# The first stage of x in 24 stores of 128 partitions, and the modes' preparation behind the second quarter's transposes

## The chip, the cores and the metric

The kernel runs on one core of one Trainium2 chip. Five engines work side by side, each with its own queue of instructions: TensorE (PE in the profile, its weight loads PEld), VectorE (DVE), ScalarE (ACT), GpSimd (POOL) and SyncE (SP). SP, ACT and POOL also issue DMA transfers. The metric is the device time of one execution in microseconds (us); the time of a kernel is the median of its runs.

## The reference, cut to what matters

The input `A_u` is one sequence of 2048 tokens with 448 channels, in float32. Two branches work on the same layer-normalised input, and their results are added to the input:

```python
xn = layernorm(x)
# branch A: a state-space model with 256 modes per channel, as a long convolution
K  = 2 * Re(sum_n C[d,n] * dt[d] * exp(A[d,n] * dt[d] * l))       # [448, 2048]
yA = irfft(rfft(xn, 4096) * rfft(K, 4096))[:2048] + xn * D_skip
# branch B: a gated unit, 448 -> 1792 -> 448
yB = (sigmoid(xn @ w_gate) * (xn @ w_up)) @ w_down
out = x + yA + yB
```

## The kernel before, in words

Tokens lie on partitions in blocks: 16 blocks `b` of 128 tokens, in four quarters of four blocks. A quarter is loaded, normalised on VectorE and ScalarE (`x_stats`, `x_scales`, `x_norm`), transposed on TensorE and split into a high part `xh` and a low part `xl` (`x_transpose`; the last 64 channels go to `xr`, whose lower half line 225 makes on VectorE). Products in float32 are made of three products of such halves. In the code `xls` holds that last line-225 instruction of the quarter transposed last.

Branch B is `glu`: for each of 14 tiles `f` of 128 hidden units and each quarter, `gate` runs 22 matmuls (line 710) into two PSUM banks `gu`, ScalarE takes the tanh (`th`), VectorE forms `hf` (line 721) and `hl` (728), ScalarE `hh` (726). A group of tiles then goes through line 823 into `po`, which line 828 adds to `acc`. The banks `gu` and `po` are four buffers in turn, so TensorE can go on only when VectorE has read an old one. The first two quarters come first ("half 0"), then the other two.

Branch A is `conv`. It runs in three stretches.

- **Preparation** (`prep`, lines 305 to 433, twice, for two halves of the channels): from the modes' parameters come powers and phases, by some 40 VectorE instructions on 112x512 tiles (for instance `ex` line 309, `fr` lines 315 and 316, a polynomial `pl` line 320) and ScalarE functions beside them.
- **The long filter** (`kgen`): 56 steps. Each makes magnitudes on GpSimd (line 520), phases on TensorE and ScalarE (`tr` line 542, `S` lines 548 to 551), products on VectorE (`Et`, `Ft`, lines 602 to 604) and 64 small matmuls (line 616). The phases are loaded 8 DMAs at a time (line 492).
- **The spectra** (`spectra`): 17 steps that load one part of the transformed x (`sx`, line 875), of the transformed filter (`skl`, 879) and a table (`tb`, 877), multiply them (`there`), transform back (`back`) and turn the result through DRAM (`v_d`, `vp`). Three loads are kept ahead (`NLD`).

The transformed x, named `x1_d` (`x_d` in the profile), is made early and kept in DRAM until the spectra. For the first two quarters `x_spec` (lines 283 to 305) makes it for two blocks at a time: four products, three copies on ScalarE, then the stores of line 301, issued on ScalarE's queue. For the other two quarters `pair_first` (lines 681 to 694) does the same with four copies (line 689) and the stores of line 691. In DRAM a block and group has its own row of 64 x 224 (`row`).

Two generators, `conv` and `glu`, are run in turn by weights, and a scheduler then sets the order on each engine by its own estimate of durations. `tc.issue_after(i)` holds instructions behind `i` in that order; `hp` raises a priority. Since the scheduler orders the whole program anew, an edit also shifts instructions far from it. Each DMA issued by SP or ACT signals one of eight semaphores, in rotation, and a new issue waits for the transfer that used that semaphore before; these are the names DMAHW0 to DMAHW7 in the order below.

Of the kernel before, what the change touches and what calls it, by code (L numbers as in the profile page):

```python
# [11 lines left out]
F32 = mybir.dt.float32  # L12
# [12 lines left out]
NB = 64  # L25
# [14 lines left out]
H = D // 2  # L40
# [8 lines left out]
LAG = 3  # L49
# [81 lines left out]
def s4d_glu_kernel(ctx, tc, io):  # L131
    nc = tc.nc
# [6 lines left out]
    dram = ctx.enter_context(tc.tile_pool(name="dram", bufs=1, space=DRAM))  # L139
    acc_d = dram.tile([128, 8, D], F32, name="acc_d")  # L140
    ph_d = dram.tile([D, 6, N], F32, name="ph_d")
    x1_d = dram.tile([2, NB, 64, H], F32, name="x1_d")

    sk_d = dram.tile([128, 2, 8, D // 64, 128], F32, name="sk_d")
    wt_d = dram.tile([2, NFT, 128, 8 * 128], F32, name="wt_d")
# [126 lines left out]
            return nc.scalar.activation(xn, xt, AF.Identity, bias=z_, scale=y_)  # L272

    def row(b, g):
        return 32 * (b // 4 % 2) + 8 * g + 4 * (b // 8) + b % 4

    def x_first_stage(to, xn, g):

        s = slice(32 * g, 32 * g + 32)
        for i in range(2):  # L280
            nc.tensor.matmul(to[64 * i : 64 * i + 64], wx[s], xn[i][s], start=True, stop=True)

    def x_spec(xn, b0):

        x1s_ = []
        for _ in range(2):
            x1s_.append(slots[("x1a", "x1b", "x1c")[x1s[0] % 3]])
            x1s[0] += 1
        ps = psc[-1].tile([128, 2, 512], F32, name="tr", bufs=1)
        kk = [psc[-1].tile([128, 512], F32, name=n, bufs=1) for n in ("ko", "kp")]  # L290
        with tc.issue_after(glu_mm[0].ins):
            for j in range(4):
                x_first_stage((ps[:, j] if j < 2 else kk[j - 2])[:, :D], xn, j)
        nc.scalar.copy(x1s_[0], ps[:, :, :D])
        for j in range(2):
            nc.scalar.copy(x1s_[1][:, j], kk[j][:, :D])
        for p in range(2):
            for i in range(2):
                r = row(b0 + i, 2 * p)
                for h in range(2):  # L300
                    nc.scalar.dma_start(
                        x1_d[h, r : r + 9 : 8].rearrange("r k d -> k r d"),
                        x1s_[p][64 * i : 64 * i + 64, :, H * h : H * h + H],
                    )
        yield 2 * WX

    def exp(ex, ki, fr, pl):
# [373 lines left out]
    def pair_first(b, xns):  # L681

        x1 = pg.tile([128, 2, D], F32, name="x1", tag="wraw", bufs=1)
        pss = [psg.tile([128, 512], F32, name="gu", bufs=4) for _ in range(4)]
        for g in range(4):
            x_first_stage(pss[g][:, :D], xns, g)
        for g in range(4):
            to = x1[:, g] if g < 2 else pg.tile([128, D], F32, name="x1", tag="rd", bufs=RB)
            nc.scalar.copy(to, pss[g][:, :D])
            for i in range(2):  # L690
                nc.scalar.dma_start(
                    x1_d[:, row(b + i, g)].rearrange("h k d -> k h d"),
                    to[64 * i : 64 * i + 64].rearrange("k (h d) -> k h d", h=2),
                )

    def gate(w, xs, to, between=None, behind=False):
        wh, wl = w
# [147 lines left out]
    def spectra(pf):  # L845
# [19 lines left out]
        def loads(h, k):  # L865
            sx = pf.tile([128, 4, H], F32, name="sx", bufs=NLD)
            sk = pf.tile([128, 7, 4, 32], F32, name="skl", bufs=NLD)
            if k == 32:

                nc.sync.dma_start(sx[:64, 0:2], x1_d[:, :, 32].rearrange("h b d -> b h d"))  # L870
                for i in range(2):
                    nc.sync.dma_start(sk[:64, :, i], sk_d[64:, i, 0, :, :32])
                return t32, sk, sx
            for i in range(2):
                nc.sync.dma_start(sx[64 * i : 64 * i + 64], x1_d[h, :, 32 * i + k : 32 * i + k + 4])
            tb = pf.tile([128, 4, 128], F32, name="tb", bufs=NLD)
            nc.sync.dma_start(tb, io["c_tab"][k // 4])

            nc.sync.dma_start(sk.rearrange("p g k e -> p g (k e)"), sk_d[:, h, k // 4])
            return tb, sk, sx  # L880
# [139 lines left out]
    def conv():  # L1020
        with tc.tile_pool(name="psk", bufs=1, space=PSUM) as ps_, tc.tile_pool(
            name="pq", bufs=1, side="right"
# [8 lines left out]
            with tc.tile_pool(name="pst", bufs=1, side="right", reuse_waits="tile") as pst:  # L1031
# [54 lines left out]
                while preps:  # L1086
                    for p in list(preps):
                        try:
                            with tc.issue_after(hfs[max(0, len(hfs) - LAG)].ins):
                                next(p)  # L1090
                        except StopIteration:
                            preps.remove(p)
                    yield WP
                    n += 1
                    if n in (2, 3):
                        if n == 2:
                            slots["x1c"] = pst.tile([128, 2, D], F32, name="x1c", tag="raw1")
                        for b in range(0, 4, 2):
                            yield from x_spec([xns[n - 2][:, b + i] for i in range(2)], 4 * (n - 2) + b)
# [11 lines left out]
    lasts, glu_mm, sp_mm, glu_on, outs, x1s, hfs, xls = [], [], [], [], [0], [0], [], []  # L1111
# [7 lines left out]
    while any(g is not None for g in gens):  # L1119
# [3 lines left out]
        i = min(live, key=lambda i: done[i] / total[i])  # L1123
# [33 lines left out]
```

## Time and profile before

| | us |
|---|---|
| median of 3 runs | 725.56 |
| lowest and highest run | 721.6, 726.61 |
| the profiled execution | 721.87 |
| its span, first to last instruction | 720.1 |

The profiled execution lies near the lowest of the three runs, 3.69 us under their median, and 1.77 us of it lie outside the span. Its mean granted TensorE clock is 0.984 of full speed. In the profile a time stands as microseconds from the start of the span; "x3" counts merged instructions; the bracket at the end of a row is how long the engine had been idle, and what ended the wait. ACTq and SPq are the queues in which ScalarE and SyncE issue DMAs.

### The profile page before, as it was taken

To read this page: it belongs to the slowest core of one execution; us is meant where nothing else is said; L and a number is where in the kernel's file an instruction comes from. 1 tells how busy PE (TensorE), PEld (TensorE's weight loads), DVE (VectorE), ACT (ScalarE), POOL (GpSimd) and SP (SyncE) were. 2 spreads that over 40 slices of the span, in tenths; PEclk is the share of its full clock that TensorE was granted. 3 is DMA by queue.
4 is the path that set the end of the run, shared out by engine and by line. 5 is a ranking of instruction groups with operands and counts; after the bars stand their busy time and mean duration, and the time that the engine had idled before them with its cause. 6 is when DMAs were issued, how large, how long until landed. Compare 5 with 4: busy or idle time off the path is not lost.

```text
span 720.1 us, 19127 instructions
## 1 busy us (share of the span) xinstructions
PE 670.9 (93%) x7752; PEld 527.3 (73%) x7752; DVE 551.4 (77%) x766; ACT 428.0 (59%) x678; POOL 371.5 (52%) x431
## 2 busy tenths in 40 slices
PE   3898999999997997989999999999999999998995
PEld 2676888877876875656888788877877777776783
DVE  5899988699899889985879889987946555546543
ACT  3655975677787789965686877777542322313320
POOL 2100147766987988885676687577833002251001
PEclk9999999999999999999999999999999999999998
DMA  9947374554254453647933344141359988899645
GB/s 208 238 118 215 97 214 154 166 159 153 64 168 140 135 135 107 178 136 203 257 112 95 95 132 128 46 140 43 86 162 319 216 235 231 253 290 228 172 131 152
DMA packets 94503, 117.23 MB, mean 163 GB/s; under 512 B 12752, under 2 KB 78288, under 8 KB 94416
## 3 DMA queue, kind: packets, MB, share of 16 engines
q1 hardware_dynamic: 65904, 91.87, 45.3%
q10 hardware_dynamic: 25936, 18.24, 9.5%
q0 software_dynamic: 2576, 5.90, 3.1%
q8 instruction: 61, 1.00, 0.6%
q14 instruction: 26, 0.21, 0.1%
HBM read 72.13 MB, written 43.84 MB: 161 GB/s over the span
## 4 chain that ended last, share of the span: by engine, by line
PE 42%; DVE 6%; ACT 4%; DMA 3%; issue 2%; SPq 1%; POOL 0%; POOLq 0%; DVEq 0%; ACTq 0%
PE gu L710 16%; PE po L823 9%; PE sp L904 6%; PE pv L931 4%; PE ko L616 4%; PE tr L542 2%; DVE Ft L604 1%; DMA sx<-x_d 1%; DVE Et L602 1%; DMA out_dram<-ac 1%; DVE Et L603 1%; PE kp L566 1%; ACT S L551 1%; ACT S L548 1%; SPq L492 1%
## 5 line engine op out<-in xcount | busy, mean ns | idle before, releaser
L520 POOL TENSOR_TENSOR me<-me,pm 128x32 f32<-128x32 f32 (+1 forms) x168 | 142.4, 848 | 73.4 <-DVE Et L603 62.1
L520 POOL TENSOR_TENSOR mf<-mf,pm 128x64 f32<-128x64 f32 (+1 forms) x112 | 119.7, 1069 | 5.9
L710 PE MATMUL gu<-xh,wh 128*128 128x512 f32 x336 | 100.0, 406 | 0.7 <-ACT xh L221 0.7
L710 PE MATMUL gu<-xh,wl 128*128 128x512 f32 x336 | 97.0, 395 | 0.0
L710 PE MATMUL gu<-xl,wh 128*128 128x512 f32 x336 | 95.8, 391 | 0.0
L602 DVE TENSOR_TENSOR Et<-me,S 128x1024 f32<-128x1024 f32 x56 | 81.8, 1461 | 17.2 <-ACT S L551 16.1
L603 DVE TENSOR_TENSOR Et<-me,S 128x1024 f32<-128x1024 f32 x56 | 78.0, 1394 | 12.6 <-ACT me L533 10.5
L823 PE MATMUL po<-dh,hh 128*128 128x448 f32 x224 | 84.2, 376 | 2.6 <-DVE hf L721 2.2
L823 PE MATMUL po<-dl,hh 128*128 128x448 f32 x224 | 82.3, 367 | 0.0
L604 DVE TENSOR_TENSOR Ft<-mf,S 128x1024 f32<-128x1024 f32 x56 | 78.1, 1394 | 5.4 <-ACT S L551 2.7
L548 ACT ACTIVATE S<-tr 128x1024 f32<-128x1024 f32 x56 | 57.6, 1028 | 40.8 <-PE tr L542 40.4
L823 PE MATMUL po<-dh,hl 128*128 128x448 f32 x224 | 81.2, 367 | 0.0
L616 PEld LDWEIGHTS ko<-Et,Ft 128*32 128x32 f32 x3584 | 55.2, 112 | 31.4 <-DVE Ft L604 13.3
L710 PEld LDWEIGHTS gu<-xh,wh 128*128 128x128 f32 x336 | 61.8, 191 | 20.1 <-issue 5.1
L616 PE MATMUL ko<-Et,Ft 128*32 128x64 f32 x3584 | 65.6, 224 | 10.8 <-DVE Ft L604 9.9
L710 PEld LDWEIGHTS gu<-xh,wl 128*128 128x128 f32 x336 | 63.8, 190 | 14.5 <-DVE hf L721 0.7
L710 PEld LDWEIGHTS gu<-xl,wh 128*128 128x128 f32 x336 | 63.4, 189 | 13.5
L726 ACT CAST hh<-hf 128x512 fp32r<-128x512 f32 x56 | 34.9, 623 | 61.8 <-DVE hf L721 57.7
L721 DVE SCALAR_TENSOR_TENSOR hf<-th,gu 128x512 f32<-128x512 f32 x56 | 38.1, 680 | 39.5 <-PE gu L710 27.1
L551 ACT ACTIVATE S<-S,hpi 128x1024 f32<-128x1024 f32 x56 | 65.5, 1170 | 0.0
L787 POOL TENSOR_TENSOR dl<-rd,dh 128x448 fp32r<-128x448 f32 x14 | 24.8, 1769 | 78.1 <-ACT dh L786 67.6
L828 DVE SCALAR_TENSOR_TENSOR acc<-po,acc 128x448 f32<-128x448 f32 x80 | 48.1, 615 | 20.7 <-PE po L823 20.4
(208 smaller groups left out, 1299.7 us busy)
## 6 DMA issues: line engine op xcount, KB each, us to landing
sk_d<-sk ACTq DMA_DIRECT2D x14, 512.0 KB
sx<-x_d SPq DMA_DIRECT2D x32, 224.0 KB
skl<-sk_d SPq DMA_DIRECT2D x16, 448.0 KB
vp<-v_d SPq DMA_DIRECT2D x16, 448.0 KB
v_d<-vt SPq DMA_DIRECT2D x14, 448.0 KB
ph<-ph_d SPq DMA_DIRECT2D x224, 24.0 KB
wt_d<-wh SPq DMA_DIRECT2D x9, 512.0 KB
wt_d<-wl SPq DMA_DIRECT2D x9, 512.0 KB
```

The costliest lines, as they stand in the source:

```text
L520: ins = nc.gpsimd.tensor_tensor(m[:, :, w + a : 2 * w : n], m[:, :, a:w:n], par(base + i).unsqueeze(2).to_broadcast([128, 4 * DC, w // n]) ...
L548: nc.scalar.activation(rows(cs), pv, AF.Abs)
L551: sins[:] = [nc.scalar.activation(cs, cs, AF.Sin, scale=-TWO_PI, bias=hpi)]
L602: v.tensor_tensor(Et[:, :, :, 32:64], two(me[:, :, 32:64]), S[:, 1::-1], ALU.mult)
L603: v.tensor_tensor(Et[:, :, :, 0:32], two(me[:, :, 0:32]), S[:, 1:3, :, ::-1], ALU.mult)
L604: fts[:] = [v.tensor_tensor(Ft, two(mf), S[:, 3:5], ALU.mult)]
L616: mm = nc.tensor.matmul(ko[32 * j : 32 * j + 32, sl], Ft[:, cc, DC * h + 4 * q + j], Et[:, cc, DC * h + 4 * q + j], start=(k == 0), stop=( ...
L710: glu_mm[:] = [nc.tensor.matmul(ps, a_, b_, start=(n == 0), stop=(n == len(mm) - 1))]
L721: marks[1] = v.scalar_tensor_tensor(hf, th, 1.0, pgu[1], ALU.add, ALU.mult)
L823: glu_mm[:] = [nc.tensor.matmul(po, a_[:, bs], w_, start=(n == 0), stop=(n == 3 * fc - 1))]
L828: v.scalar_tensor_tensor(acc[:, b], po, 0.5, acc[:, b], ALU.mult, ALU.add)
L904: mm = nc.tensor.matmul(to, tb[:kk, t, 64 * c : 64 * c + 64], rhs, start=True, stop=True, skip_group_check=True,)
```

## The change

Three things are changed.

1. **The stores.** `x1_d` gets another layout, [8, 2, 8, 64, 224]. The two blocks of one call now lie next to each other, so one transfer takes all 128 partitions. `x_spec` issues 2 transfers in place of 8 per call (4 calls: 8 in place of 32), `pair_first` 4 in place of 8 per call (4 calls: 16 in place of 32).
2. **The loads.** A load of the spectra still brings 64 rows of 3,584 bytes, but those rows lie in DRAM as 8 groups of 8 in place of 64 at one step. The one load of step 32 becomes two.
3. **The queueing.** All of `prep` is now also held behind `xls[0]`, which is line 225 of the second quarter when `prep` is recorded.

```diff
-    x1_d = dram.tile([2, NB, 64, H], F32, name="x1_d")
+    x1_d = dram.tile([8, 2, 8, 64, H], F32, name="x1_d")
...
     def row(b, g):
-        return 32 * (b // 4 % 2) + 8 * g + 4 * (b // 8) + b % 4
+        return 4 * (b // 4 % 2) + g, 4 * (b // 8) + b % 4
...
         for p in range(2):
-            for i in range(2):
-                r = row(b0 + i, 2 * p)
-                for h in range(2):
-                    nc.scalar.dma_start(
-                        x1_d[h, r : r + 9 : 8].rearrange("r k d -> k r d"),
-                        x1s_[p][64 * i : 64 * i + 64, :, H * h : H * h + H],
-                    )
+            g, r = row(b0, 2 * p)
+            nc.scalar.dma_start(
+                x1_d[g : g + 2, :, r : r + 2].rearrange("g h i k d -> (i k) (g h) d"),
+                x1s_[p].rearrange("p g (h d) -> p (g h) d", h=2),
+            )
...
-            for i in range(2):
-                nc.scalar.dma_start(
-                    x1_d[:, row(b + i, g)].rearrange("h k d -> k h d"),
-                    to[64 * i : 64 * i + 64].rearrange("k (h d) -> k h d", h=2),
-                )
+            q, r = row(b, g)
+            nc.scalar.dma_start(
+                x1_d[q, :, r : r + 2].rearrange("h i k d -> (i k) h d"), to.rearrange("p (h d) -> p h d", h=2)
+            )
...
-                nc.sync.dma_start(sx[:64, 0:2], x1_d[:, :, 32].rearrange("h b d -> b h d"))
+                for i in range(2):
+                    nc.sync.dma_start(sx[:64, i], x1_d[:, i, :, 32])
...
-                nc.sync.dma_start(sx[64 * i : 64 * i + 64], x1_d[h, :, 32 * i + k : 32 * i + k + 4])
+                fr = x1_d[:, h, :, 32 * i + k : 32 * i + k + 4]
+                nc.sync.dma_start(sx[64 * i : 64 * i + 64], fr.rearrange("g r k d -> g r (k d)"))
...
-                            with tc.issue_after(hfs[max(0, len(hfs) - LAG)].ins):
+                            with tc.issue_after(hfs[max(0, len(hfs) - LAG)].ins), tc.issue_after(xls[0].ins):
```

The changed file is a line shorter, so most of its later lines stand two or three numbers lower: `hf` of line 721 is 718 there, `hl` of 728 is 725, `pl` of 320 is 318.

**VectorE at the second quarter.** In the kernel before, `prep` (`ex`, `fr`) stands between the parts of the second quarter (`xl`, `xr`):

```order
L721 SCALAR_TENSOR_TENSOR hf<-th,gu 128x512
L309 TENSOR_SCALAR ex<-ex,lim 112x514 x2
L728 TENSOR_TENSOR hl<-hf,hh 128x512
L721 SCALAR_TENSOR_TENSOR hf<-th,gu 128x512
L315 SCALAR_TENSOR_TENSOR fr<-ki,ex 112x514 x2
L222 TENSOR_TENSOR xl<-tr,xh 128x512
L316 SCALAR_TENSOR_TENSOR fr<-ki,fr 112x514
L222 TENSOR_TENSOR xl<-ko,xh 128x512
L316 SCALAR_TENSOR_TENSOR fr<-ki,fr 112x514
L222 TENSOR_TENSOR xl<-kp,xh 128x512
L225 TENSOR_TENSOR xr<-gu,xr 64x512
```

The same place on VectorE in the changed kernel:

```order
L718 SCALAR_TENSOR_TENSOR hf<-th,gu 128x512
L725 TENSOR_TENSOR hl<-hf,hh 128x512
L718 SCALAR_TENSOR_TENSOR hf<-th,gu 128x512
L222 TENSOR_TENSOR xl<-tr,xh 128x512
L222 TENSOR_TENSOR xl<-ko,xh 128x512
L222 TENSOR_TENSOR xl<-kp,xh 128x512
L225 TENSOR_TENSOR xr<-gu,xr 64x512
L248 BN_STATS st_84<-xe_116 128x6 x4
L248 BN_STATS st_84<-xe_118 128x6 x3
L725 TENSOR_TENSOR hl<-hf,hh 128x512
L248 BN_STATS st_84<-xe_118 128x6
L307 TENSOR_SCALAR ex<-ex,lim 112x514 x2
```

Four `fr` instructions no longer stand ahead of `xr`, and the two of `ex` have moved behind the statistics of the next blocks.

**VectorE some 30 us later.** The fifth `hf` of the program, in the kernel before, has ten `pl` of line 320 ahead of it, the last two right here:

```order
L326 RECIPROCAL m_391<-m_391 112x128 x4
L320 SCALAR_TENSOR_TENSOR pl<-pl,fr 112x514 x2
L260 SCALAR_TENSOR_TENSOR z<-z,ve 128x8
L764 TENSOR_TENSOR wl<-wraw,wh 128x1024
L721 SCALAR_TENSOR_TENSOR hf<-th,gu 128x512
L374 TENSOR_TENSOR w_380<-w_380,m_379 112x512
```

In the changed kernel the fifth `hf` stands here:

```order
L259 TENSOR_TENSOR z<-ys 128x8
L318 SCALAR_TENSOR_TENSOR pl<-pl,fr 112x514
L324 RECIPROCAL m_391<-m_391 112x128
L318 SCALAR_TENSOR_TENSOR pl<-pl,fr 112x514
L718 SCALAR_TENSOR_TENSOR hf<-th,gu 128x512
L372 TENSOR_TENSOR w_380<-w_380,m_379 112x512
```

Seven `pl` stand ahead of it now, three fewer; the rest of what stands ahead is the same but for two of the short `z`.

**ScalarE in the middle of the program**, where `pair_first` stores the third quarter's second pair. Before (the names in brackets are what an instruction waits for):

```order
L691 DMA x_d<-x_3792 64x2x224 [waits DMAHW6_49,Activation_49]
L691 DMA x_d<-x_3792 64x2x224 [waits DMAHW0_49]
L626 COPY ks<-ko 128x512 [waits PE_49]
L551 ACTIVATE S_1119<-S_1119,hpi 128x2x512 [waits Activation_49]
L691 DMA x_d<-x_3792 64x2x224 [waits DMAHW2_49]
L691 DMA x_d<-x_3792 64x2x224 [waits DMAHW4_49]
L689 COPY x_3811<-gu 128x448 [waits DMAHW7_49,DMAHW1_49]
L689 COPY x_3815<-gu 128x448 [waits DMAHW5_49,PE_49]
L218 CAST xh<-gu 128x2x256 [waits PE_49]
L691 DMA x_d<-x_3811 64x2x224 [waits DMAHW0_49,Activation_49]
L691 DMA x_d<-x_3811 64x2x224 [waits DMAHW2_49]
L221 CAST xh<-gu 128x256 [waits PE_49]
```

The same place on ScalarE in the changed kernel:

```order
L689 DMA x_d<-x_3764 128x2x224 [waits Activation_49]
L689 DMA x_d<-x_3764 128x2x224 [waits DMAHW4_49,Activation_49]
L549 ACTIVATE S_1095<-S_1095,hpi 128x2x512 [waits Activation_49]
L687 COPY x_3781<-gu 128x448 [waits DMAHW3_49,PE_49]
L687 COPY x_3784<-gu 128x448 [waits PE_49]
L689 DMA x_d<-x_3781 128x2x224 [waits DMAHW2_49,Activation_49]
L689 DMA x_d<-x_3784 128x2x224 [waits DMAHW4_49,Activation_49]
L218 CAST xh<-gu 128x2x256 [waits PE_49]
L221 CAST xh<-gu 128x256 [waits PE_49]
L723 CAST hh<-hf 128x512 [waits DVE_49]
```

Half of the issues are gone, and no store stands between the two `xh` copies any more.

## The prediction

> **What bounds the kernel now.** I read the page first, then busy times by stretch, then the gaps of TensorE and what ended each. The page, with the busy sums and three rows of tenths:
>
> ```profile
> PE 670.9 (93%) x7752; PEld 527.3 (73%) x7752; DVE 551.4 (77%) x766; ACT 428.0 (59%) x678; POOL 371.5 (52%) x431
> PE   3898999999997997989999999999999999998995
> DVE  5899988699899889985879889987946555546543
> DMA  9947374554254453647933344141359988899645
> ```
>
> TensorE is busy for 93% of the span. Of the other 49 us, the first slice (3 tenths of 18 us) and the last (5) hold some 12 and 9, the start and the end. What is left for any edit is some 28 us in gaps, and VectorE is nearly as full as TensorE over the first twenty slices. DMA is full from slice 30 on, in the spectra. The stretches that the change touches, by busy time of PE, PEld, DVE, ACT, POOL, then clock, DMA share and GB/s:
>
> ```profile
> 30.00:63.00 33.00, 28.84 (x158) 19.60 (x158) 32.94 (x65) 15.27 (x27) 2.48 (x3) 0.95 0.62 159
> 44.00:75.00 31.00, 28.66 (x160) 21.28 (x159) 30.76 (x60) 19.63 (x44) 1.34 (x2) 1.00 0.70 191
> 280.00:340.00 60.00, 56.22 (x839) 37.46 (x838) 49.54 (x62) 46.60 (x78) 45.73 (x53) 0.94 0.57 161
> 590.00:599.00 9.00, 9.00 (x72) 7.13 (x68) 4.76 (x10) 2.03 (x4) 0.00 (x0) 1.00 0.87 233
> 640.00:660.00 20.00, 16.75 (x163) 12.11 (x163) 7.89 (x16) 3.83 (x8) 6.77 (x7) 1.00 0.97 261
> ```
>
> From 30 to 63 VectorE is the full engine (32.94 of 33 us), not TensorE. From 280 to 340, where `pair_first` works, TensorE idles 60 - 56.22 = 3.78 us. In a round of the spectra TensorE is full and DMA is at 0.87.
>
> **The queueing.** VectorE's rows around the second quarter, with `prep` (`ex`, `fr`) between its parts, and those that lead to the fifth `hf`:
>
> ```profile
> 25.09 1.00 DVE L309 TENSOR_SCALAR ex<-ex,lim 112x514 f32<-112x514 f32 x2
> 27.04 0.69 DVE L728 TENSOR_TENSOR hl<-hf,hh 128x512 fp32r<-128x512 f32 x1 [0.96 <-ACT hh L726]
> 29.55 0.69 DVE L721 SCALAR_TENSOR_TENSOR hf<-th,gu 128x512 f32<-128x512 f32 x1 [1.82 <-PE gu L710]
> 30.16 1.29 DVE L315 SCALAR_TENSOR_TENSOR fr<-ki,ex 112x514 f32<-112x514 int32 x2
> 31.36 0.68 DVE L222 TENSOR_TENSOR xl<-tr,xh 128x512 fp32r<-128x512 f32 x1
> 34.48 0.68 DVE L225 TENSOR_TENSOR xr<-gu,xr 64x512 fp32r<-64x512 f32 x1
> ...
> 60.62 1.24 DVE L320 SCALAR_TENSOR_TENSOR pl<-pl,fr 112x514 f32<-112x514 f32 x2
> 61.77 0.17 DVE L260 SCALAR_TENSOR_TENSOR z<-z,ve 128x8 f32<-128x8 f32 x1
> 62.98 0.69 DVE L721 SCALAR_TENSOR_TENSOR hf<-th,gu 128x512 f32<-128x512 f32 x1
> ```
>
> TensorE's gaps that go with them, and two later ones:
>
> ```profile
> 30.11 2.35 PE L710 MATMUL gu<-xh,wh 128*128 128x512 f32 x9 [0.65 <-ACT xh L221]
> 35.22 0.79 PE L710 MATMUL gu<-xr,wh 128*128 128x512 f32 x1 [2.77 <-DVE xr L225]
> 63.72 0.47 PE L823 MATMUL po<-dh,hh 128*128 128x448 f32 x1 [1.89 <-DVE hf L721]
> 316.75 0.44 PE L212 MATMUL gu<-ident,xt 128*128 128x128 f32 x2 [0.94 <-DVE xr L225]
> 318.04 1.21 PE L616 MATMUL ko<-Et,Ft 128*32 128x64 f32 x40 [0.85 <-DVE Et L602]
> ```
>
> The order takes four `fr` from ahead of `xr`. They cost 31.36 - 30.16 = 1.20 us for two, so 2.4 us for four, and `xr` starts at 32.1 in place of 34.48. TensorE then resumes at about 32.8 in place of 35.22: 2.4 us sooner. The 0.65 us ahead of it goes too, but it is not a gain of its own, since `xr` ends the wait.
>
> That gain does not last. TensorE next waits for the fifth `hf` (1.89 us at 63.72), and VectorE reaches it through a stretch in which it is never free. What stands ahead of this `hf` changes little. Three `pl` go behind it: 3 x 0.6 (1.24 for two) = -1.8 us. The two `ex` (1.00) took time in which VectorE otherwise waited (0.96 and 1.82 in the rows); now they stand inside the full stretch: +1.0. Two more `z` start ahead of it, about 0.1 us each by their spacing: +0.2. Sum -0.6, say -0.7 with the short ones between. So `hf` starts near 62.3, and TensorE, ready 2.4 us earlier, waits the longer. I book **-0.7 us**.
>
> What is queued behind the new wait is `prep` itself, and behind that the filter. The first `tr` (line 542) now stands 17 rows of `po` later on TensorE. These rows, in the kernel before:
>
> ```profile
> 112.07 0.36 PE L823 MATMUL po<-dh,hh 128*128 128x448 f32 x1
> 112.27 0.36 PE L823 MATMUL po<-dl,hh 128*128 128x448 f32 x1
> ...
> 113.69 0.62 PE L542 MATMUL tr<-sel,ph 128*128 128x512 f32 x2
> ```
>
> A row is 0.20 us, so the filter starts 17 x 0.20 = 3.4 us later against the other branch. TensorE has `po` work to put in its place, and that is the cover: at nothing while it lasts, at up to +3.4 us if the filter's chain sets the pace later. The bounds of this edit are -2.4 - 0.65 = -3.1 and +3.4; -0.7 is what the next wait leaves.
>
> **The stores.** Issues on the chip, by line (shortest, median, longest in ns, first and last start), from the view of the tile `x_d`:
>
> ```profile
> L691 ACTq DMA_DIRECT2D x_d<-x x32: 582/600/2543, 281.6 to 334.6; - x32
> L875 SPq DMA_DIRECT2D sx<-x_d x32: 450/581/1093, 514.5 to 669.0; - x32
> L301 ACTq DMA_DIRECT2D x_d<-x1ab x24: 582/614/1673, 44.3 to 73.7; - x24
> L301 ACTq DMA_DIRECT2D x_d<-x1c x8: 582/683/1182, 51.7 to 64.4; - x8
> ```
>
> In `x_spec` 24 issues go, some 24 x 0.61 = 15 us of ScalarE's queue. ScalarE is busy 19.63 of 31 us there, and the one long gap of TensorE (63.72) ends on VectorE. So I book 0. Without VectorE's lateness it would be worth part of that gap, 1.89 us at most.
>
> In `pair_first` 16 issues go, 16 x 0.60 = 9.6 us of the queue. Here the issues do hold ScalarE up, and at the spectra's end other issues do the same:
>
> ```profile
> 305.19 2.54 ACTq L691 DMA_DIRECT2D x_d<-x  x1
> 307.77 0.37 ACT L221 CAST xh<-gu 128x256 fp32r<-128x256 f32 x1 [2.33 <-PE po L823]
> ...
> 641.17 6.69 ACTq L240 DMA_DIRECT2D out_dram<-ac  x3
> 647.91 0.60 ACT L718 ACTIVATE th<-gu 128x512 f32<-128x512 f32 x1 [11.53 <-DMA out_dram<-ac]
> 650.36 0.98 PE L904 MATMUL sp<-skl,tb 128*64 128x224 f32 x8 [2.61 <-ACT vt L937]
> ```
>
> The issue at 305.19 lasts 2.54 us where 0.60 is the median, and `xh` starts when it ends; the order shows that such an issue waits for one of the eight transfers in flight. In the changed order no store stands between the two `xh`. TensorE's gaps at 316.75 and 318.04 end on VectorE instructions that follow such `xh` and copies. Bounds: 0, if VectorE (49.54 of 60 us) would be late anyway, and -3.78, all the idle time. I take the two gaps with rows, 0.94 + 0.85: **-1.8 us**. A transfer is now twice as large or four times, and lands later; that waits on the same eight, and there are fewer.
>
> **The loads.** Issue and bytes stay; SyncE gets one issue more at 520.7, ahead of an instruction whose wait lasts to 537: nothing. What can change is how fast a load runs. The DMA rate within one round, when the turned result `vp` runs, then `sx`, then stores and `skl` (last column):
>
> ```profile
> 582.50:583.20 0.70, 0.70 (x12) 0.52 (x8) 0.00 (x0) 0.69 (x2) 0.00 (x0) 1.00 1.05 347
> 584.00:586.40 2.40, 2.40 (x19) 1.84 (x16) 2.37 (x6) 0.53 (x1) 0.00 (x0) 1.00 1.03 210
> 587.40:589.40 2.00, 2.00 (x14) 1.63 (x14) 0.93 (x2) 0.00 (x0) 0.00 (x0) 1.00 1.04 418
> ```
>
> The two `sx` of a round (448 KB) already run at 210 GB/s, half of the 418 that the next ones reach. What holds them there the trace does not say. If it is the memory or the port, a new pattern served by half as many engines at their full speed runs at 418 / 2 = 209: the same. I take **0**, the nearest row. Bounds: -3.25, if shorter queues end the stall at 650 and the one behind it (20 - 16.75), and +14 (below).
>
> The Trainium skill ("DMA: Bandwidth & Descriptors", section "Why a DMA increments its semaphore by 16 and not by 1") says that a transfer uses the largest number of engines up to 16 that divides the slowest dimension on both sides. By that rule the new loads, 8 groups on one side and 64 rows on the other, go to 8 engines in place of 16. It speaks against this change. With those engines at full speed the sum would stay as it is; at the speed that the loads have now the time would be that of the second rival. No row here shows a load with 8 groups.
>
> **The sum.** -0.7 - 1.8 + 0 = -2.5 us. Against the profiled execution that is 721.87 - 2.5 = 719.4. Its time lies 3.69 us under the median of the runs; on the median's side it is 725.56 - 2.5 = **723**.
>
> **The rivals.**
>
> *All gaps close.* If VectorE's stretch to 63 isn't kept full, for instance because the order's tail of `prep` waits elsewhere, the second quarter keeps 2.4 us. If the stores were the whole cause at 280 to 340, 3.78 go, and with shorter queues the 3.25 at 640 to 660. Sum -9.4: 716. For it: each gap has a row. Against it: three of the five releasers are VectorE, whose work is the same.
>
> *The loads run at half the rate*, the case on the other side. Place: the rounds from 537 to 700. Two `sx` take 2.4 us of a round; at half the rate 4.8. A round of 9.0 us has 0.87 x 9.0 = 7.8 us of DMA, and would have 10.2, against TensorE's 9.0: DMA would set the pace. It decides once the loads cost 1.2 us more per round. Price: at most 1.2 x 16 = 19; the loads run three steps ahead, which hides the first few, so 12 rounds x 1.2 = +14. 725.56 - 2.5 + 14 = 737. For it: DMA is full from 537 on. Against it: the loads run at half rate already.
>
> *The later filter sets the pace.* 3.4 us later, less 1.8: 725.56 + 3.4 - 1.8 = 727. For it: VectorE is nearly as full as TensorE until 300. Against it: `po` fills TensorE.
>
> **How the numbers follow.** My forecast 0.45, its own range 718 to 728 (the sum's -2.5 with some 5 us for waits that the new order moves). All gaps close 0.20; half rate 0.18; later filter 0.17. A measurement of this kernel can tell about 1% (7.3 us) from no change: its three runs spread over 5. Faster by over 1% (under 718.3) has all of 0.20 and 0.05 of the forecast: 0.25. Slower by over 1% (over 732.8) has 0.18 and 0.04 of the later filter: 0.22. Within: 0.53. The range 713 to 738 takes in 716 and 737 and leaves the ends beyond them.
>
> **What would show it.** In the changed profile `xr` should start near 32 and TensorE resume near 33, and the gap at the fifth `hf` should grow from 1.89 to about 3.6, ending near 63. Store issues should number 24, near 0.6 us each, with no 2 us idle before `xh`. TensorE's idle time from 280 to 340 should fall from 3.78 to about 2. In the spectra a round should stay at 9 us. Wrong would be: a round longer than 9.5 us with TensorE waiting for `sx`; a gap at 63 that shrinks; or new gaps over 3 us between 120 and 530, where I hold the new order to be as good as the old.

## The result and the profile after

The changed kernel took 750.9 us (median of 4 runs, 750.55 to 752.35), the kernel before 723.58 us (4 runs beside it). The ratio is 1.0395, interval 1.0356 to 1.0435: 4% slower, where 723 was forecast and 738 was the end of the range. The profiled execution has a span of 748.8 us against 720.1, so 28.7 us are to be found.

The page of the changed kernel, with the same four rows as before:

```profile
PE 677.6 (90%) x7752; PEld 532.7 (71%) x7752; DVE 554.0 (74%) x766; ACT 428.0 (57%) x678; POOL 359.8 (48%) x431
PE   3998999998997996999999999999999998667995
DVE  5799896699798999597589879879555554224543
DMA  9955174454154434549633323321698788787655
```

TensorE is busy 6.7 us longer with the same 7,752 matmuls, and idle for 748.8 - 677.6 = 71.2 us against 49.2. Its new holes lie in slices 35 to 37, in the spectra, where DMA has fallen from 8 and 9 to 7 and 8 although the transfers are the same. So the spectra's transfers take longer and yet leave DMA engines idle. One stretch shows it, the third of these (columns as in the prediction's tables of stretches; the last three are clock, DMA share, GB/s):

```profile
30.00:63.00 33.00, 28.36 (x157) 18.15 (x155) 32.94 (x66) 16.40 (x28) 2.52 (x3) 0.99 0.73 202
280.00:340.00 60.00, 51.46 (x757) 33.37 (x757) 50.43 (x57) 46.28 (x79) 44.06 (x51) 0.91 0.47 150
594.00:595.00 1.00, 1.00 (x6) 0.94 (x5) 1.00 (x3) 0.00 (x0) 0.00 (x0) 1.00 0.50 204
```

The third row is a microsecond at the end of a round: half of the 16 DMA engines are busy (0.50), and 204 GB/s flow. The second row is where `pair_first` works: TensorE idles 60 - 51.46 = 8.54 us there, not the 2 that were forecast. The first row still has VectorE full.

TensorE's rows after some of its larger gaps, in order of time:

```profile
33.02 0.50 PE L707 MATMUL gu<-xr,wh 128*128 128x512 f32 x1 [1.08 <-DVE xr L225]
59.61 0.97 PE L281 MATMUL kp<-xn,wx 32*64 32x448 f32 x4 [1.28 <-ACT x1c L296]
63.20 0.74 PE L820 MATMUL po<-dh,hh 128*128 128x448 f32 x1 [2.22 <-DVE hf L718]
176.57 0.65 PE L614 MATMUL ko<-Et,Ft 128*32 128x64 f32 x31 [2.48 <-DVE Ft L602]
235.67 1.22 PE L540 MATMUL tr<-sel,ph 128*128 128x512 f32 x2 [5.47 <-ACT S L548]
295.51 1.72 PE L614 MATMUL ko<-Et,Ft 128*32 128x64 f32 x56 [3.69 <-DVE Ft L602]
639.23 1.76 PE L903 MATMUL sp<-skl,tb 128*64 128x224 f32 x8 [3.80 <-DMA tb<-in_c_tab_dram]
652.01 1.12 PE L903 MATMUL sp<-skl,tb 128*64 128x224 f32 x8 [3.52 <-issue]
677.92 1.76 PE L903 MATMUL sp<-skl,tb 128*64 128x224 f32 x8 [9.65 <-ACT vt L936]
```

The first three are those of the second quarter. The next three lie in the long filter, which now starts later. The last three lie in the spectra. At 639.23 TensorE waits for the table `tb`, a transfer that SyncE issues right behind the two loads of `sx`; the profile names nothing for the wait at 652.01. The last, 9.65 us, is the place of the 2.61 us before (650.36), almost four times as long.

Three stretches hold the 28.7 us. The row of `tr` gives the first and the last start of the filter's phases on TensorE, here before and then after:

```profile
L542 PE MATMUL tr<-sel,ph x112: 388/398/797, 113.7 to 519.9; 128*128 128x512 f32 x112
```

```profile
L540 PE MATMUL tr<-sel,ph x112: 389/398/794, 119.4 to 527.8; 128*128 128x512 f32 x112
```

The filter starts 5.7 us later, is 408.4 - 406.2 = 2.2 us longer, and what follows its last `tr` takes 748.8 - 527.8 = 221.0 us in place of 200.2: 20.8 us more. That last part, before and then after:

```profile
519.90:720.10 200.20, 186.50 (x1693) 142.25 (x1691) 104.28 (x196) 53.54 (x99) 41.56 (x54) 0.99 0.81 216
```

```profile
527.80:748.80 221.00, 191.44 (x1693) 146.08 (x1691) 102.87 (x197) 53.32 (x99) 42.25 (x55) 0.95 0.75 198
```

TensorE idles 29.6 us there in place of 13.7, 15.9 more, and takes 4.9 us longer for the same matmuls, at a mean clock of 0.95 in place of 0.99.

Two of the prediction's rivals have come true together: by these two executions the loads have 20.8, and the later filter 7.9. The second number is rough. Kernels of the next section that keep the order of before have their last `tr` anywhere between 519.9 and 524.4.

A round of the spectra, read from the issues of the turned result `vp` on SyncE's queue, before and after:

```profile
580.27 0.56 SPq L953 DMA_DIRECT2D vp<-v_d  x1
...
589.20 0.56 SPq L953 DMA_DIRECT2D vp<-v_d  x1
...
598.07 0.57 SPq L953 DMA_DIRECT2D vp<-v_d  x1
```

```profile
594.94 0.58 SPq L952 DMA_DIRECT2D vp<-v_d  x1
...
605.74 0.58 SPq L952 DMA_DIRECT2D vp<-v_d  x1
...
616.89 0.58 SPq L952 DMA_DIRECT2D vp<-v_d  x1
```

8.9 us a round before, 10.8 and 11.2 after. And ScalarE at the spectra's end, where it issues three stores of the result:

```profile
668.27 7.14 ACTq L240 DMA_DIRECT2D out_dram<-ac  x3
675.46 0.60 ACT L715 ACTIVATE th<-gu 128x512 f32<-128x512 f32 x1 [18.72 <-DMA sx<-x_d]
```

The name in the bracket is the point: a store of the result waits for the semaphore that a load of `sx` holds, since the eight semaphores go round over both queues. In the trace the first and the third of these stores wait for semaphores that loads of `sx` took, issued at 657.29 and 663.52. ScalarE does nothing for 18.72 us, and TensorE waits with it for 9.65.

### The profile page after: what moved, and what is told of

It is laid out like the page before. It is cut to its first block, busy times and chain, and to the rows that moved or that the text cites. A ratio compares the mean times of both kernels' runs of the same rounds, so it can differ in the third digit from the quotient of the medians.

```text
span 748.8 us, 19090 instructions
## 1 busy us (share of the span) xinstructions
PE 677.6 (90%) x7752; PEld 532.7 (71%) x7752; DVE 554.0 (74%) x766; ACT 428.0 (57%) x678; POOL 359.8 (48%) x431
## 2 busy tenths in 40 slices
DMA packets 93607, 117.22 MB, mean 157 GB/s; under 512 B 11856, under 2 KB 77392, under 8 KB 93520
## 4 chain that ended last, share of the span: by engine, by line
PE 51%; DVE 17%; DMA 10%; ACT 9%; issue 5%; SPq 4%; POOL 3%; DVEq 0%; ACTq 0%; POOLq 0%
PE gu L707 20%; PE po L820 11%; PE sp L903 6%; PE ko L614 5%; PE tr L540 3%; PE pv L930 3%; DMA tb<-in_c_tab_dram 2%; DVE Ft L602 2%; DVE Et L601 2%; DMA sx<-x_d 2%; DVE hl L725 2%; DVE Et L600 1%; DMA v_d<-vt 1%; DVE pm L454 1%; POOL me L518 1%
## 5 line engine op out<-in xcount | busy, mean ns | idle before, releaser
L518 POOL TENSOR_TENSOR me<-me,pm 128x32 f32<-128x32 f32 (+1 forms) x168 | 140.6, 837 | 87.2 <-DVE Et L601 78.7
L518 POOL TENSOR_TENSOR mf<-mf,pm 128x64 f32<-128x64 f32 (+1 forms) x112 | 113.8, 1016 | 6.0
L602 DVE TENSOR_TENSOR Ft<-mf,S 128x1024 f32<-128x1024 f32 x56 | 80.6, 1439 | 2.7 <-PE ko L614 1.4
L614 PEld LDWEIGHTS ko<-Et,Ft 128*32 128x32 f32 x3584 | 55.1, 112 | 31.8 <-issue 13.7
L718 DVE SCALAR_TENSOR_TENSOR hf<-th,gu 128x512 f32<-128x512 f32 x56 | 38.1, 680 | 50.6 <-PE gu L707 28.5
L707 PEld LDWEIGHTS gu<-xl,wh 128*128 128x128 f32 x336 | 63.2, 188 | 13.7
L715 ACT ACTIVATE th<-gu 128x512 f32<-128x512 f32 x56 | 33.6, 601 | 60.8 <-PE gu L707 41.7
```

The source lines that it names most:

```text
L518: ins = nc.gpsimd.tensor_tensor(m[:, :, w + a : 2 * w : n], m[:, :, a:w:n], par(base + i).unsqueeze(2).to_broadcast([128, 4 * DC, w // n]) ...
L602: fts[:] = [v.tensor_tensor(Ft, two(mf), S[:, 3:5], ALU.mult)]
L614: mm = nc.tensor.matmul(ko[32 * j : 32 * j + 32, sl], Ft[:, cc, DC * h + 4 * q + j], Et[:, cc, DC * h + 4 * q + j], start=(k == 0), stop=( ...
L707: glu_mm[:] = [nc.tensor.matmul(ps, a_, b_, start=(n == 0), stop=(n == len(mm) - 1))]
L718: marks[1] = v.scalar_tensor_tensor(hf, th, 1.0, pgu[1], ALU.add, ALU.mult)
```

## The experiments

Sixteen kernels were run. Ratios are against the kernel before on the same chip, with their 95% intervals.

### The loads: 8 groups, 16 groups, 4 groups

**Run e3_groups8** is the kernel before with a gap in memory behind every eighth row (and, as in the changed kernel, two loads in place of one in step 32):

```diff
-    x1_d = dram.tile([2, NB, 64, H], F32, name="x1_d")
+    x1_d = dram.tile([2, 8, 9, 64, H], F32, name="x1_d")
...
-                nc.sync.dma_start(sx[64 * i : 64 * i + 64], x1_d[h, :, 32 * i + k : 32 * i + k + 4])
+                fr = x1_d[h, :, :8, 32 * i + k : 32 * i + k + 4]
+                nc.sync.dma_start(sx[64 * i : 64 * i + 64], fr.rearrange("g r k d -> g r (k d)"))
```

> The kernel before with one thing changed: the rows of x_d in memory stand in 8 groups of 8 with a gap behind each group, so that a load of sx has 8 groups of 8 rows in place of 64 evenly spaced rows; stores and order are those of before (one load more of the last frequency). Theory 'eight engines': each such load is served by 8 engines, the spectra get about 20 us longer, and nothing ahead of them changes: 743 us (738 to 748), with 16 x 16 = 256 packets fewer of the small kind (one load of 16 becomes two of 8, 32 loads lose 8 each), rounds near 10.6 us in place of 9 and a long wait of ScalarE's out_dram issue. Rival 'order': the spectra's loss comes from the other order of instructions and issues; then this kernel takes what before takes, 722 to 727.

Measured: 746.74 us, ratio 1.0335 (1.0279 to 1.0392). The instructions of all engines stand in the order of the kernel before, and still the spectra take 222.3 us from the last `tr` on.

**Run e4_groups16** is the same with `[2, 16, 5, 64, H]` and 16 groups of 4 rows.

> As the run with 8 groups, but the rows stand in 16 groups of 4, again with a gap behind each group: the memory is as scattered and the pattern has as many dimensions, only the number of groups differs. Theory 'eight engines': 16 groups go to 16 engines as the 64 rows did: 722 to 727 us, as before. Rival 'pattern': an interrupted pattern of rows is slow by itself, whatever the number of groups: about 743 us.

Measured: 722.06 us, ratio 0.9987 (0.9953 to 1.0021). So it is not gaps in memory, the extra dimension or the second load of step 32. It is the number of groups.

The page's count of small packets tells how many engines served a load, since each engine that takes part in a transfer writes its semaphore once. Before, and then with 8 and with 4 groups:

```profile
DMA packets 94503, 117.23 MB, mean 163 GB/s; under 512 B 12752, under 2 KB 78288, under 8 KB 94416
...
q1 hardware_dynamic: 65904, 91.87, 45.3%
```

```profile
DMA packets 94247, 117.22 MB, mean 157 GB/s; under 512 B 12496, under 2 KB 78032, under 8 KB 94160
...
q1 hardware_dynamic: 65648, 91.87, 44.0%
```

```profile
DMA packets 94111, 117.22 MB, mean 151 GB/s; under 512 B 12360, under 2 KB 77896, under 8 KB 94024
...
q1 hardware_dynamic: 65512, 91.87, 42.3%
```

With 8 groups 12752 - 12496 = 256 small packets are missing, 32 loads x 8. With 4 groups 392, which is 32 x 12 and 8 for step 32. The changed kernel has 11856, which is 896 fewer: the same 256, and 16 for each of the 40 stores saved. This is what the Trainium skill ("DMA: Bandwidth & Descriptors", section "Why a DMA increments its semaphore by 16 and not by 1") says of the number of engines, and the trace agrees to the packet.

The same lines hold the reason for the loss. The share of SyncE's queue q1 times 16 engines times the span is the time that its packets took on all engines: 0.453 x 16 x 720.1 = 5,219 us before, 0.440 x 16 x 744.8 = 5,243 us with 8 groups. In sum the packets did not get shorter when half as many engines carried the loads. So the same work lies on fewer engines. The other transfers of a round are spread over all 16 and wait behind it on those, as the wait for `tb` above shows, and the free engines idle, as the share of 0.50 shows.

**Run e11_groups4** carries it one step further, with 4 groups of 16 rows.

> The kernel before with the rows of x_d in 4 groups of 16. Theory 'as many engines as groups, and a packet takes as long as before' (some 0.27 us): the two loads of a round put 32 packets on each of 4 engines, 32 x 0.27 = 8.6 us, with some 5.4 us of the round's other packets 14 us in place of 9: about 16 x 5 = 80 us more, 790 to 815 us, and 32 x 4 packets of the small kind fewer again than with 8 groups. Rival 'a total rate is shared, packets run at 0.14 us when fewer engines pull': 4.5 + 5.4 = 9.9 us a round, 735 to 745 us. Rival 'no fewer than 8 engines': as with 8 groups, 747 us.

Measured: 777.04 us, ratio 1.0726 (1.065 to 1.0803), between the two expectations. A round of the full stretch is (629.38 - 588.71) / 3 = 13.6 us by the issues of `vp`, near the 14 of the first theory. But only 57.5 / 4.7 = 12 rounds' worth of it is paid in the spectra (257.7 us in place of 200.2), not 16. And at the end of a round the four engines run alone, and fast:

```profile
599.00:601.50 2.50, 0.99 (x11) 0.94 (x13) 0.00 (x0) 0.00 (x0) 0.00 (x0) 1.00 0.25 100
```

A quarter of the DMA engines is busy and moves 100 GB/s, 25 each, as the eight above (204 / 8). So the rival was right about packets that run alone, and wrong about the round. Two runs of this kernel were made.

### What holds a load of 64 partitions at 210 GB/s

The prediction left this open. Two kernels look at it; both leave out the right rows of x, so that the spectra multiply others. **Run e9_sx_from_filter** reads the same shape from another place:

```diff
-                nc.sync.dma_start(sx[64 * i : 64 * i + 64], x1_d[h, :, 32 * i + k : 32 * i + k + 4])
+                fr = sk_d[64 * i : 64 * i + 64, h, k // 4].rearrange("p g d -> p (g d)")
+                nc.sync.dma_start(sx[64 * i : 64 * i + 64].rearrange("p k d -> p (k d)"), fr)
```

> Both loads of sx take their 64 rows of 3,584 bytes from sk_d, the memory that skl is loaded from, at the same step, in place of x_d (so the spectra use wrong data for x). What holds a packet of sx at some 0.29 us: theory 'where it is read from': they fall to 0.14, the stretch of sx runs at 400 GB/s. Rival 'the 64 partitions it is written to, or what runs beside it': 0.29 and 210 GB/s stay. The time hardly tells it (TensorE is full in a round): 718 to 726 us.

**Run e10_sx_one_load** reads from the same place in one load for all 128 partitions:

```diff
-            for i in range(2):
-                nc.sync.dma_start(sx[64 * i : 64 * i + 64], x1_d[h, :, 32 * i + k : 32 * i + k + 4])
+            fr = x1_d[:, :, 32 * h + k : 32 * h + k + 4].rearrange("h r k d -> (h r) (k d)")
+            nc.sync.dma_start(sx.rearrange("p k d -> p (k d)"), fr)
```

> One load of 128 rows of x_d for all 128 partitions of sx in place of two of 64 (the rows are those of both halves of the channels, so the spectra use wrong data for x). If the 64 partitions hold a packet at 0.29 us, it falls to 0.14 here; if it is where it is read from or what runs beside it, 0.29 stays. Time 718 to 726 us.

Measured: 726.87 and 722.35 us, one execution each, so the time tells nothing, as expected. The stretch of `sx` in the first, and the stretch in the second when `vp` has ended:

```profile
598.00:600.00 2.00, 2.00 (x15) 1.53 (x12) 1.97 (x5) 0.53 (x1) 0.00 (x0) 1.00 1.15 212
```

```profile
601.00:602.40 1.40, 1.40 (x19) 1.00 (x14) 1.09 (x3) 0.42 (x2) 0.00 (x0) 1.00 0.93 315
```

From another place the two loads still run at 212 GB/s, so it is not the place that is read. With one load of 128 partitions in their place the stretch, which has packets of `tb` too, reaches 315. That leaves the 64 partitions of a load, or its being one of two; no run tells these apart. The Trainium skill ("SBUF — State Buffer", section "Door 1: The DMA port swizzle (why `[64,N]` ≈ `[32,N]`)") gives a reason of the first kind: partitions 0 to 63, or 64 to 127, are reached through 8 of 16 ports, some 218 GB/s. The 210 and 212 measured here agree with that.

### The stores and the queueing, one at a time

**Run e1_queue_alone**: only the queueing, in the kernel before.

```diff
-                            with tc.issue_after(hfs[max(0, len(hfs) - LAG)].ins):
+                            with tc.issue_after(hfs[max(0, len(hfs) - LAG)].ins), tc.issue_after(xls[0].ins):
```

> The queueing alone in the kernel before; stores, layout and loads of sx as before. Theory 'later filter': the 8 us that the changed kernel loses ahead of the spectra come from the filter that starts some 3.4 us later, and the waits of TensorE for S and Ft that follow: 730 to 733 us. Rival 'stores move ScalarE': the queueing costs nothing by itself (the -0.7 of the prediction): 722 to 726 us.

Measured: 734.85 us, ratio 1.018 (1.0105 to 1.0254). **Run e2_stores_alone** is the changed kernel without that line.

> The 24 stores and the new layout without the queueing. Theory 'eight engines' gives +20 us in the spectra; with 'later filter' the part ahead of the spectra is that of before or a little better: 741 to 745 us. Rival 'stores move ScalarE': the 8 us ahead of the spectra are the stores' too: 749 to 752 us. If the spectra's loss were the queueing's: 724.

Measured: 742.91 us, ratio 1.0281 (1.0221 to 1.0341). The queueing costs by itself, and the stores with their layout cost by themselves, and both are slower.

**Run e5_even_rows** gives the changed kernel a layout in which a load is 64 rows at one step again. One transfer can't take both halves of the channels then, so `x_spec` needs 4 per call, 32 stores in all:

```diff
-    x1_d = dram.tile([8, 2, 8, 64, H], F32, name="x1_d")
+    x1_d = dram.tile([2, 8, 8, 64, H], F32, name="x1_d")
...
+            for h in range(2):
+                nc.scalar.dma_start(
+                    x1_d[h, g : g + 2, r : r + 2].rearrange("g i k d -> (i k) g d"),
+                    x1s_[p][:, :, H * h : H * h + H],
+                )
```

> The changed kernel with another layout: the two halves of the channels outermost, so that a load of sx is 64 rows at one step again; x_spec needs 4 transfers per call in place of 2 (32 stores in all); the queueing stays. Theory 'eight engines': the spectra's 20 us are gone, and what is left over the time before is the queueing less the stores' gain: 728 to 734 us, rounds of 9 us. Rival 'large stores': what slows the spectra is what the larger stores leave behind: 745 to 751 us.

Measured: 734.78 us, ratio 1.0134 (1.0072 to 1.0195); the spectra take 199.2 us. **Run e6_even_noqueue** is the same without the queueing.

> The same without the queueing: 32 stores of 128 partitions, loads of 64 rows at one step, order of preparation as before. The prediction's term for the stores is -1.8: 721.5 us (719 to 723.5). Rival 'stores are neutral': 723 to 725. Rival 'stores cost': over 726.

Measured: 718.5 us, ratio 0.9938 (0.9911 to 0.9965). This version beats both kernels, the one before by 0.6%. A part of its gain lies in the stretch of `pair_first` and the issues there:

```profile
280.00:340.00 60.00, 57.76 (x847) 37.56 (x846) 54.59 (x64) 51.02 (x85) 47.13 (x55) 0.95 0.56 170
```

```profile
L690 ACTq DMA_DIRECT2D x_d<-x x16: 366/376/1490, 284.3 to 332.7; - x16
```

TensorE idles 60 - 57.76 = 2.24 us there, in place of 3.78. An issue's median is 0.376 us in place of 0.600, and the longest 1.49 in place of 2.54.

By these ratios, on 723 us: 8 groups cost 24.2, the queueing 13.0, the stores bring 4.5. The sum, 32.7, stands against 28.5 measured for all three. It is the queueing that doesn't add: on top of run e2 it costs 8.2 (1.0395 - 1.0281), and with that the sum is 27.9. It also delays less there: the first `tr` of the changed kernel has 109 rows of `po` ahead of it, that of the queueing alone 129, and that of before 92.

### The later filter

Is the queueing's price the filter's later start, or what it does on VectorE? **Run e7_late_filter** moves the start without queueing, by a weight that takes the two generators' turns:

```diff
-WP = 5
+WP = 5.6
```

> The kernel before with the weight of a step of preparation at 5.6 in place of 5, and no queueing: VectorE's parts of the second quarter stand as before, but the filter's first tr on TensorE has 125 rows of po ahead of it in place of 92, as with the queueing alone (129), 33 x 0.2 = 6.6 us. Theory 'later filter': the delay alone costs what the queueing cost: 731 to 736 us. Rival 'VectorE's order': the cost comes from what the queueing does on VectorE between 30 and 64 us: 722 to 726 us.

Measured: 739.88 us, ratio 1.023 (1.017 to 1.0291). **Run e8_queue_early_filter** has the queueing and `WP = 4.4`.

> The queueing alone, with the weight of a step of preparation at 4.4: the filter's first tr has 92 rows of po ahead of it again, as in the kernel before, and the eighth 153 in place of 171. Theory 'later filter': the loss is gone: 721 to 727 us. Rival 'VectorE's order': it stays: 732 to 737 us.

Measured: 727.66 us, ratio 1.0079 (1.0045 to 1.0113): most of the loss is gone. **Run e12_even_early** is e6_even_noqueue with `WP = 4`.

> The 32 stores with loads of 64 rows and no queueing (718.5 us), with the weight of a step of preparation at 4 in place of 5: the filter's first tr has 72 rows of po ahead of it in place of 88, and the eighth 144 in place of 171. Theory 'the filter's start sets the end, its length stays near 406': it starts 16 x 0.2 = 3.2 us sooner, and the time is 713 to 717 us. Rival 'preparation isn't ready sooner, VectorE is full': 718 to 722 us.

Measured: 737.13 us, ratio 1.0176 (1.0128 to 1.0224), the opposite of what was expected. The filter's times, each of one profiled execution, show why weights are a poor knife:

| kernel | first `tr` | last `tr` | between | after it |
|---|---|---|---|---|
| before | 113.7 | 519.9 | 406.2 | 200.2 |
| e4_groups16 | 116.1 | 523.9 | 407.8 | 197.0 |
| e3_groups8 | 116.3 | 522.5 | 406.1 | 222.3 |
| e6_even_noqueue | 114.0 | 514.9 | 400.9 | 199.6 |
| e16_queue_second_half | 113.9 | 523.5 | 409.6 | 199.2 |
| changed | 119.4 | 527.8 | 408.4 | 221.0 |
| e13_delay_small | 119.3 | 527.0 | 407.7 | 199.3 |
| e14_delay_large | 123.0 | 526.7 | 403.6 | 199.8 |
| e15_queue_first_half | 126.7 | 530.8 | 404.1 | 200.1 |
| e1_queue_alone | 126.3 | 533.8 | 407.5 | 199.7 |
| e5_even_rows | 127.0 | 534.3 | 407.3 | 199.2 |
| e8_queue_early_filter | 116.9 | 523.2 | 406.3 | 204.2 |
| e7_late_filter | 120.6 | 539.8 | 419.1 | 197.4 |
| e12_even_early | 114.0 | 531.0 | 417.0 | 204.4 |

The rows of e4 and e3 have the order of before and still start some 2.5 us later, so a step of that size between two rows says nothing by itself. In e12 the first `tr` had 16 rows of `po` fewer ahead of it than in e6, but it started at 114.0 all the same. It did not wait for its inputs: TensorE's wait for the fifth `hf` ends at 67.42 there (63.52 in e6), and from 70.36 to 114.0 TensorE works without a wait. And both e7 and e12 have a filter 11 to 16 us longer, since the weight also changes what else stands inside it. So e7 proves nothing about the start alone.

**Runs e13_delay_small and e14_delay_large** come nearer: GpSimd clears the phase tiles three, or six, times in place of once, and nothing is queued. VectorE's first 202 instructions, up to 114 us, keep the order of before.

```diff
         for t in pht:
-            nc.gpsimd.memset(t.bitcast(F32), 1.0)
+            for _ in range(3):
+                nc.gpsimd.memset(t.bitcast(F32), 1.0)
```

> The kernel before, with GpSimd's two writes that clear the phase tiles done three times each; nothing is queued. The filter's first tr has 111 rows of po ahead of it in place of 92: 19 x 0.2 = 3.8 us (109 in the changed kernel). Theory 'the filter's start sets the end': at least these 4 us more, and up to 8 with what the changed kernel lost: 727 to 732 us. Rival 'VectorE's order is the cost of the queueing': 721 to 726 us.

> The same with six writes each: 127 rows of po ahead (129 with the queueing alone), 35 x 0.2 = 7.0 us. Theory 'start': as much as the queueing alone, 730 to 737 us. Rival 'VectorE's order': 721 to 726 us.

Measured: 730.76 us, ratio 1.0096 (1.0066 to 1.0126), and 730.65 us, ratio 1.0123 (1.0057 to 1.019). Two or five extra clears of each tile cost 7 to 9 us. In both, TensorE waits in the same three places as in the changed kernel, and for the same releasers; here is the second:

```profile
176.23 1.10 PE L617 MATMUL ko<-Et,Ft 128*32 128x64 f32 x64 [2.47 <-DVE Ft L605]
...
235.33 1.22 PE L543 MATMUL tr<-sel,ph 128*128 128x512 f32 x2 [5.65 <-ACT S L551]
...
295.15 1.94 PE L617 MATMUL ko<-Et,Ft 128*32 128x64 f32 x64 [2.75 <-DVE Ft L605]
```

These three are 10.9 us together. Before, and in e4, e6 and e16 (below), two waits stand in their place, of some 3.4 us near 230 and 2.8 to 3.0 near 280, and that is 6.2 us in the kernel before.

**Runs e15_queue_first_half and e16_queue_second_half** split the queueing by the two halves of the channels (`p` is one half's preparation):

```diff
+                            xl = tc.issue_after(xls[0].ins) if p is all_[0] else nullcontext()
-                            with tc.issue_after(hfs[max(0, len(hfs) - LAG)].ins):
+                            with tc.issue_after(hfs[max(0, len(hfs) - LAG)].ins), xl:
```

> The queueing for the first half of the channels only: 130 rows of po ahead of the first tr. Theory 'start': as the whole queueing, 731 to 738 us. Rival 'VectorE's order': about half of its cost, 726 to 731 us.

> The queueing for the second half of the channels only: 88 rows of po ahead of the first tr, four fewer than in the kernel before. Theory 'start': as before or a little better, 720 to 725 us. Rival 'VectorE's order': 726 to 731 us, as with the first half.

Measured: 733.62 us, ratio 1.0148 (1.0094 to 1.0203), and 723.34 us, ratio 1.0 (0.9968 to 1.0031). The half that delays the first `tr` (126.7) costs about what the whole costs; the half that doesn't (113.9) costs nothing. Both queue VectorE's work, though the second moves less of it: 28 of VectorE's 766 instructions leave the order of before, against 110.

What stays open: the two delays cost the same within their intervals, though one is nearly twice the other (19 and 35 rows of `po`). Behind the first 202 they give VectorE the same order but for 2 instructions, and that order differs from the one of before in 59. So a later start and the order that the scheduler makes behind it come together, and no run has one without the other. The delays also cost less (7 to 9) than the queueing (13, interval 7.6 to 18.4). In the three kernels that queue the early half and start the filter at 126 us or later (e1, e15 and e5) TensorE has one gap more, of 3.28, 3.37 and 2.16 us; the delays and the changed kernel don't have it. The row of e1:

```profile
120.35 0.66 PE L823 MATMUL po<-dh,hh 128*128 128x448 f32 x1 [3.28 <-DVE acc L828]
```

Here VectorE, late with its preparation, holds a bank of `po`. It may be the rest; no run took it away alone.

## Why the prediction was wrong, point by point

**The second quarter was right.** `xr` was to start at 32.1 and TensorE to resume at 32.8; the fifth `hf` near 62.3, with the gap ending near 63. VectorE's rows after:

```profile
32.29 0.68 DVE L225 TENSOR_TENSOR xr<-gu,xr 64x512 fp32r<-64x512 f32 x1
...
62.48 0.67 DVE L718 SCALAR_TENSOR_TENSOR hf<-th,gu 128x512 f32<-128x512 f32 x1
```

32.29, 33.02, 62.48 and 63.20. Of 0.65 + 2.77 + 1.89 = 5.31 us of gaps up to 64 us, 1.08 + 1.28 + 2.22 = 4.58 are left: -0.73, where -0.7 was booked. That agreement is in part luck: the first matmuls of the two executions already start 0.46 us apart (12.28 and 12.74). And the gap at `hf` grew to 2.22, not to 3.6, because 1.28 us of waiting came in ahead of it, at 59.61, for ScalarE's `x1c`. But the 2.4 us were given back before `hf`, as the step said.

**The step that failed there is the bound behind it.** The prediction had the later filter "at nothing while it lasts, at up to +3.4 us if the filter's chain sets the pace later", with `po` as the cover. The cover doesn't hold: with the first `tr` 19 or 35 rows of `po` later and VectorE's order unchanged up to there, the kernel takes 7 to 9 us more, and in the changed kernel the queueing costs 8.2 us. The delay itself was sized about right. Between the two profiled executions it is 5.7 us and not 3.4, but the clock ahead of the filter differs between them. It was full in the one before. It is 0.96 in the changed kernel and 0.95 in e4, whose instructions stand in the order of before. Before, e4 and after:

```profile
64.00:120.00 56.00, 55.67 (x265) 47.78 (x265) 50.09 (x89) 46.08 (x92) 17.75 (x21) 1.00 0.56 162
```

```profile
64.00:120.00 56.00, 55.88 (x253) 48.11 (x254) 48.99 (x88) 46.11 (x92) 17.74 (x22) 0.95 0.56 163
```

```profile
64.00:120.00 56.00, 55.48 (x253) 47.42 (x253) 49.54 (x87) 41.35 (x86) 15.36 (x19) 0.96 0.45 134
```

56 x 0.04 = 2.2 us, and 3.4 + 2.2 = 5.6. This fall need not be an effect of the change: in all five kernels with the order of before up to the spectra (e3, e4, e9, e10, e11) the clock of this stretch is 0.94 to 0.97, and the first `tr` starts at 115.0 to 116.3. Against these the changed kernel is 3.1 to 4.4 us late. What follows is not one for one: the three waits inside the filter (176, 236 and 296 us) take their part, whatever the delay. New gaps over 3 us between 120 and 530 were a sign of being wrong that the prediction had named, and 5.47 and 3.69 came.

**The stores were right in sign and place, and too small.** -1.8 was booked, with TensorE idle for about 2 us from 280 to 340. Run e6_even_noqueue, with 32 stores of this kind and no queueing, shows 2.24 us there and 4.5 us less in all (interval 2.5 to 6.4). Where the rest of the 4.5 lies no run shows. In the changed kernel the same stretch idles 8.54 us, since the filter's waits have moved into it. A price per issue was wrong: 0.60 us was taken for the new issues, and they take 0.37. The issues after:

```profile
L874 SPq DMA_DIRECT2D sx<-x_d x32: 572/584/686, 523.2 to 697.5; - x32
L689 ACTq DMA_DIRECT2D x_d<-x x16: 366/366/1232, 290.5 to 343.0; - x16
L299 ACTq DMA_DIRECT2D x_d<-x1ab x6: 367/386/425, 41.9 to 66.1; - x6
L299 ACTq DMA_DIRECT2D x_d<-x1c x2: 366/370/373, 51.3 to 59.6; - x2
```

**The step that failed most is the loads, booked at 0: they cost 24.2 us of the 28.5.** "A new pattern served by half as many engines at their full speed runs at 418 / 2 = 209: the same. I take 0, the nearest row." Each half of it is true by itself: eight engines served it, and alone they moved 204 GB/s. What the step left out is what else stands on those engines, and so the wait of TensorE for it. A rate that is the same for the transfer is not the same for the queues: before, 16 engines each gave the two loads some 8 packets of a round, now 8 engines give 16 each, and the transfers that go to all 16 end when those eight do. The trace of before showed that the engines were not free for it (DMA 0.87 in a round).

**The rival had the mechanism, and its price was too small.** It put the extra at 1.2 us a round, 10.2 in place of 9.0, for 12 rounds: +14. The round came out at 10.8 to 11.2, some 2 us more than 8.9, and the spectra at 20.8 us more. In the terms of TensorE that is 15.9 us more of waiting, 7.0 of them where 2.61 grew to 9.65 while ScalarE's stores wait for a load of `sx`, and 4.9 us for the same matmuls at a lower clock. The sign that the prediction had named, a round over 9.5 us, came, though TensorE waits for `tb` behind the loads and not for `sx` itself. The rival was given 0.18, with "the loads run at half rate already" against it. That was no argument against it.

**The two rivals add.** They were priced apart, 737 and 727, and no case had both. Added at their own prices they give 725.56 - 1.8 + 3.4 + 14 = 741. The rest is size: 24.2 us for the loads and 8.2 for the queueing.

## What to carry to other kernels

Before a DRAM layout is changed to save stores, write down the access pattern of every load that reads it back: an outermost dimension of 8 in place of 64 took half of the DMA engines from a load, and that cost 24 us where the stores saved 4.5. A transfer on fewer engines is priced by the fullest engine of the round, its other transfers included, not by its own rate. And where a long chain follows, other work that an engine can put ahead of the chain's first instruction is not a cover for its delay: price it by a run that delays this instruction, and look at the order that the scheduler makes behind it.

## What the runs showed of the hardware

- Two loads into 64 partitions each run at 210 GB/s, and at 212 when read from another buffer; with one load into 128 in their place the stretch runs at 315.
- An issue of a store from 128 partitions takes ScalarE's queue 0.37 us, and one from 64 partitions, with a half or a quarter of the bytes, 0.60 us.
- The number of engines behind a transfer can be read from the page: 256 small packets fewer for 32 loads is 8 engines fewer each.
- Eight DMA engines that run such loads alone move 204 GB/s, and four move 100; in a round with other transfers the same loads made the kernel 3.35% and 7.3% slower.
- A clear of a 128x512 tile takes GpSimd 0.52 us, so the four extra clears of run e13 are 2.1 us of its time; the kernel took 7 us of 723 more (interval 4.8 to 9.1), and in its order 19 more rows of `po` stand ahead of the filter's first `tr`.
